# Three pieces' first FFN product by Strassen's seven block products, later maxima through DRAM, outputs waiting in the raw weights' buffer

## The chip, the cores and the metric

The kernel runs on one core of a Trainium2 chip. The metric is the time of one execution on the device, in microseconds; the median of three runs is 985.28 us (984.22 to 986.99). The profile is of one execution that took 982.83 us, of which 981.0 us are the span from its first to its last profiled instruction.

## The reference

Block-causal attention over 8 batches, 8 heads, 576 positions and head size 64, followed by a feed-forward network (FFN) on all 4608 tokens of width 512 with 2048 hidden columns:

```python
scores = scale * np.matmul(q, k.transpose(0, 1, 3, 2))
scores = np.where(block_i >= block_j, scores, -1000000000.0)
...
attn = attn / (np.sum(attn, axis=-1, keepdims=True) + 1e-09)
x = np.matmul(attn, v)
...
h = x @ w_in
g = h * np.clip(h + 3.0, 0.0, 6.0) / 6.0
return (g @ w_out).astype(np.float32)
```

## The kernel before

All of it is float32 in and out. To use TensorE's float16 rate, each operand is scaled by a power of two and split into a high and a low float16 half; a product is then three float16 products, high by high, high by low and low by high. A tensor's scale comes from its largest absolute value (`pow2_scale`, line 561). Where the maximum has to be taken over all 128 partitions (`exact`), TensorE turns the column of 128 maxima into a row (tile `mt`), VectorE (DVE) reduces it, and a second small matmul (tile `mb`) spreads the result again. This is done for each of 8 weight chunks (`w_max`, line 678) and for v of each of the 8 batches (`v_max`, line 747).

The tokens are cut into 13 pieces (line 1141), numbered 0 to 12, and a piece from 4 on has 384 tokens. Piece 0 is computed in float32. For every piece the FFN runs over 16 groups f of 128 hidden columns:

- `ffn1_` (line 1246) makes h of one f in a PSUM tile `h`: 4 depths by 3 products, each as a pair of matmuls of 64 weight columns that run side by side, so 24 matmuls of 384 columns. ScalarE (ACT) then writes `r` (a Relu), DVE multiplies, ACT writes the high half of `g` and DVE its low half.
- `ffn2_` (line 1302) adds g of one f to three PSUM accumulators `o`, 18 matmuls of 512 columns. After f = 15, the sums are scaled into tiles `osb` and stored.

Attention works on 32 pairs of heads (n). A pair is loaded, scaled and split, transposed by a DMA (`qkT`), and goes through scores (`s`), softmax on DVE and ACT (`st`, `p`, `ph`, `phl`), DMA transposes of the probabilities (`pT`), and `pv` (`pv_group`, line 1157), whose result is split into the `x` of a piece. All 4 pairs of a batch feed the pieces of that batch, so pieces 10 to 12 take batches 6 and 7.

The order of the work comes from a planner. The kernel's calls don't issue instructions; a `Recorder` (line 85) collects operations with their dependences, and each operation has a key, the time at which it is due. The keys come from tables at the top of the file: `AT` gives the due time of each attention pair, `FT` that of each FFN piece. `schedule` (line 289) then lists the operations for each engine, the smallest key first among those that could run, and chooses ACT or DVE where either can do a step (`scaled` with "AV"). The engines run these fixed lists in order. A tile whose tag has `bufs` buffers waits until an earlier tile of the tag has had its last reader.

Names that the steps below use: `raw` is the one buffer (tag `raw`, 4 KB in each partition) into which weights are loaded; `stage` has 4 buffers for short-lived tiles; `g` has 4 buffers (`NGB`); `win` holds the split weights of the first product. All operations are recorded by helpers, so that the profile gives line L491 for nearly all of them, and tiles tell them apart.

Of the kernel before, what the change touches and what calls it, by code (L numbers as in the profile page):

```python
# [8 lines left out]
F16 = mybir.dt.float16  # L9
BF16 = mybir.dt.bfloat16  # L10
# [39 lines left out]
RS, RL, VL1 = 2.209, 24.843, 24.11  # L50
VM0, VMX = 49.529, 0.186
AT = ((4, 86.25), (6, 123.23), (8, 163.76), (9, 178.32), (10, 200.46), (12, 251.25), (14, 297.48), (15, 319.97), (16, 344.82), (24, 581.69), (32, 825.86))
FT = ((0, 34), (1, 120), (2, 165.28), (3, 233.86), (4, 274.28), (5, 355.06), (7, 504.5), (10, 755.22), (13, 989.58))
UNI = False
QP = 0.558
VP = 0.387
BLK = 64
# [23 lines left out]

ADV = {("tensor", "a"): 99.24}


class Recorder:
# [11 lines left out]
    LOADS = 95.0  # L97
    BIAS = {"vector": 250.0, "gpsimd": 500.0}
    EDGE = 0.0
    BURST, PATIENCE = 3, 4000.0  # L100

    def __init__(self, nc):
        self.nc = nc
        self.ops = []
        self.key = 0.0
        self.cls = ""
        self.joint = None
        self.adv = ADV
        for n in self.NAMES:
# [6 lines left out]
    def box(a):  # L116
        sz = mybir.dt.size(a.dtype)
# [58 lines left out]
    def add(self, ways):  # L176
# [20 lines left out]
        for i, (a, w) in enumerate([(a, False) for a in ins] + [(a, True) for a in outs]):  # L197
            if self.on_chip(a):
                self.touch(op, a, w, self.LOAD[mybir.dt.size(a.dtype)] if eng == "tensor" and not i else 1.0)
# [295 lines left out]
def kernel(  # L495
# [39 lines left out]
    E_X = 2.0 ** -14  # L535
    E_G = 2.0 ** -27
    C_EXP = (D ** -0.5) * 2.0 ** -28
    C_H = 2.0 ** -28
    C_O = 2.0 ** -15 / 6.0
    TINY = 1e-18  # L540
# [5 lines left out]
    attp = ctx.enter_context(tc.tile_pool(name="att", bufs=2))  # L546
    ffp = ctx.enter_context(tc.tile_pool(name="ff", bufs=3))
    ps_s = ctx.enter_context(tc.tile_pool(name="ps_s", bufs=3, space=bass.MemoryType.PSUM))
    ps_h = ctx.enter_context(tc.tile_pool(name="ps_h", bufs=2, space=bass.MemoryType.PSUM))
# [10 lines left out]

    def pow2_scale(mx, n, nm, to=None, exact=False):
# [8 lines left out]
        if exact:  # L570
            pt_ = ps_s.tile([P, 512], F32, tag="s", name=f"mt_{nm}")
            nc.joint = "mt", nm
            for h in range(2):
                wide = mx[:, h % n:h % n + 1].to_broadcast([P, BLK])
                nc.tensor.matmul(pt_[h * BLK:(h + 1) * BLK, :P], wide, ident, start=True, stop=True)
            nc.joint = None
            dg = sm.tile([P, n + 1], F32, tag=f"dg{n}", name=f"dg_{nm}")
            nc.vector.tensor_reduce(dg[:, n:], pt_[:, :P], axis=AX.X, op=ALU.max)
            nc.vector.tensor_scalar_mul(dg[:, :n], ident[:, :(n - 1) * BLK + 1:BLK], dg[:, n:])
            mx = dg[:, :n]  # L580
        ps = ps_s.tile([P, 512], F32, tag="s", name=f"mb_{nm}")
        nc.joint = "mb", nm
        for h in range(2):
            nc.tensor.matmul(ps[h * BLK:(h + 1) * BLK, :n], ones[:, :BLK], mx, start=True, stop=True)
        nc.joint = None
        nc.vector.tensor_scalar_max(am, ps[:, :n], TINY)
# [52 lines left out]
    def w_load(w, c, half):  # L639
# [36 lines left out]
        )  # L676

    def w_max(c):

        acc = sm.tile([P, 2, 2], F32, tag="wacc", bufs=2, name=f"wacc{c}")  # L680
        for wi, w in enumerate("io"):
            for half in range(2):
                c32 = w_f32(w, c, half)
                ab = ffp.tile([P, WC], F32, tag="stage", bufs=NST_B, name=f"ab{w}{c}_{half}")
                ab = ab.rearrange("p (r l n) -> p r l n", r=c32.shape[1], l=2)
                nc.scalar.activation(ab, c32, AF.Abs, accum_out=acc[:, wi, half:half + 1])
        m = sm.tile([P, 2], F32, tag="wm", name=f"wm{c}")
        nc.vector.tensor_reduce(m, acc, axis=AX.X, op=ALU.max)
        pow2_scale(m, 2, f"w{c}", (pwio[:, c], rsio[:, c]), exact=True)

    def w_split(c):

        rs = rsio[:, c]
        for wi, w in enumerate("io"):
            for half in range(2):
                c32 = w_f32(w, c, half)
                part = w_part(w, c, half)
                hi, lo = (part[:, :, i].rearrange("p r (l n) -> p r l n", l=2) for i in range(2))
                nc.scaled(hi, c32, rs[:, wi:wi + 1], "AVP")
                nc.vector.scalar_tensor_tensor(  # L700
                    lo, c32, rs[:, wi:wi + 1], hi, op0=ALU.mult, op1=ALU.subtract
                )

# [43 lines left out]
    def v_max(n):  # L747
# [8 lines left out]
        if hp == NPAIR - 1:  # L756
            m1 = sm.tile([P, 1], F32, tag="vm1", name=f"vm1_{b}")
            nc.vector.tensor_reduce(m1, vmax[b], axis=AX.X, op=ALU.max)
            vscale[b] = pow2_scale(m1, 1, f"v{b}", exact=True)

# [11 lines left out]

    def h_scale(b):

        if b not in hs:
            t = sm.tile([P, NCH], F32, tag="sh", bufs=3, name=f"sh{b}")
# [3 lines left out]
            nc.vector.tensor_scalar_mul(t, t, C_H)  # L780
            hs[b] = t
        return hs[b]

# [373 lines left out]
    def pv_group(n, g):  # L1157
# [88 lines left out]
    def ffn1_(pc, f):  # L1246
        if pc == 0:
            return ffn1_f32(f)
        x, w, fc = xb[pc % 4], width(pc), f * P % NH
        ps = ps_h.tile([P, TP], F32, tag="h", name=f"h{pc}_{f}")  # L1250
# [51 lines left out]
    def ffn2_(pc, f):  # L1302
# [34 lines left out]
        for t, a in enumerate(acc.pop(pc)):  # L1337
            n, half = min(w - t * P, P), w - t * P < P
            o = ffp.tile([P, DM], F32, tag="stage", bufs=NST_B, name=f"osb{pc}_{t}")
            oc = o[:, :DM // 2] if half else o  # L1340
            ac = a[:, :DM // 2] if half else a
            nc.scaled(oc, ac, so[:, t:t + 1] if pc else 1.0 / 6.0, "AV")
            rows = out[row + t * P:row + t * P + n]
            if half:
# [16 lines left out]
    def ffn_step(lim):  # L1361

        nonlocal done1, done2
        if done1 < lim:
            if done1 >= NFT:
                need(done1 % NFT // 2)
            while len(n_raw) < min(4 * (done1 // 2 + 1), 4 * NCH):
                w_ops.pop(0)()
            ffn1(*divmod(done1, NFT))
            done1 += 1  # L1370
# [59 lines left out]
    for n in range(NPAIR):  # L1430
        t = RT[n]
        at(t - QR, qk_load32_rest, n, lead=RL - QR)
        at(t - QR, qk_prep32, n, 1)
        at(AS[3] + 0.1 + 0.1 * n, v_max, n)
# [93 lines left out]
```

## Time and profile before

| | before |
|---|---|
| median of 3 runs | 985.28 us (984.22 to 986.99) |
| the profiled execution | 982.83 us |
| its span | 981.0 us |
| TensorE (PE) busy | 964.2 us, 98% |
| DVE busy | 756.4 us, 77% |
| ACT busy | 696.5 us, 71% |
| granted TensorE clock, mean | 0.999 |

PE is TensorE's matmuls, PEld its weight loads, SP the engine that issues DMAs, POOL GpSimd. A group's row gives its count, its busy time, the mean duration of one in ns, and behind the second bar the idle time of its engine just before it, with what ended that. The views by windows give each engine's busy time in a stretch; the timeline and the chain give the start, the length and the count of merged instructions. Durations of back-to-back instructions overlap a little, so a count times a duration can be longer than the busy time.

### The profile page before, as it was taken

How to read it: one execution, taken by the hardware profiler on the slowest of the kernel's cores; microseconds unless marked ns; L12 is line 12 of the kernel's file. 1: busy time of each engine (PE TensorE's matmuls, PEld its weight loads, DVE VectorE, ACT ScalarE, POOL GpSimd, SP SyncE). 2: the span in 40 equal slices, each digit the busy share in tenths (PEclk: the TensorE clock that was granted, in tenths of full speed). 3: DMA queues.
4: the chain of work that ended last, by engine and by line, in shares of the span. 5: the costliest groups of instructions: out<-in, count | busy, mean ns of one | idle time of the engine just before them, and what ended most of it. 6: DMA issues, size and time to landing. Idle time of an engine off the chain costs nothing.

```text
span 981.0 us, 29087 instructions
## 1 busy us (share of the span) xinstructions
PE 964.2 (98%) x11754; PEld 722.9 (74%) x11754; DVE 756.4 (77%) x2081; ACT 696.5 (71%) x1840; POOL 28.3 (3%) x109
## 2 busy tenths in 40 slices
PE   8999999999999999999999999999999999999998
PEld 6655447877778867777777677777777777777776
DVE  6889998999989999999999898899886432332331
ACT  6899789778778888888878788787775433333332
POOL 3012000000000000000000000000000000000000
PEclk9999999999999999999999999999999999999999
DMA  6966689899898899898899898786664200000000
GB/s 141 277 204 223 159 154 178 169 183 189 155 173 148 149 175 157 170 162 148 161 186 177 151 188 156 132 164 131 108 133 77 36 34 1 1 33 1 34 2 33
DMA packets 414199, 128.91 MB, mean 131 GB/s; under 512 B 403184, under 2 KB 403440, under 8 KB 414064
## 3 DMA queue, kind: packets, MB, share of 16 engines
q1 hardware_dynamic: 414064, 127.05, 66.5%
q8 instruction: 92, 1.51, 0.6%
q14 instruction: 43, 0.35, 0.1%
HBM read 45.09 MB, written 9.44 MB: 56 GB/s over the span
## 4 chain that ended last, share of the span: by engine, by line
PE 58%; DVE 6%; DMA 2%; ACT 1%; issue 1%; DVEq 0%; ACTq 0%
PE o L491 25%; PE h L491 25%; PE s L491 4%; PE pv L491 4%; DMA pT<-ph 2%; DVE st L491 1%; DVE phl L491 1%; DVE ph L491 1%; DVE r L491 1%; DVE g L491 1%; DVE qks L491 1%; DVE vhl L491 0%; ACT p L491 0%; DVE x L491 0%; ACT r L491 0%
## 5 line engine op out<-in xcount | busy, mean ns | idle before, releaser
L491 PE MATMUL h<-x,win 128*64 128x384 f16 (+3 forms) x4790 | 440.7, 319 | 4.4 <-DVE r L491 4.4
L491 PE MATMUL o<-wout,g 128*64 128x512 f16 (+2 forms) x3424 | 432.3, 383 | 0.0
L491 PEld LDWEIGHTS <-win 128*64 128x64 f16 x4608 | 296.1, 110 | 62.5 <-issue 6.5
L491 PEld LDWEIGHTS <-g 128*64 128x64 f16 x3264 | 219.2, 110 | 91.6
L491 ACT ACTIVATE r<-h,eg,sh 128x192 f32<-128x192 f32 (+1 forms) x240 | 134.1, 580 | 115.2 <-PE h L491 110.8
L491 DVE SCALAR_TENSOR_TENSOR r<-r,eg,h 128x384 f32<-128x384 f32 (+1 forms) x192 | 110.3, 575 | 132.0 <-ACT r L491 131.3
L491 ACT ACTIVATE p<-s,st,esc 128x64 f32<-128x64 f32 (+1 forms) x280 | 163.1, 586 | 13.6 <-DVE ph L491 7.3
L491 DVE SCALAR_TENSOR_TENSOR g<-r,g 128x384 f16<-128x384 f32 (+1 forms) x192 | 99.5, 519 | 34.1 <-ACT g L491 33.3
L491 DVE TENSOR_REDUCE st<-s 128x1 f32<-128x64 f32 (+1 forms) x280 | 119.2, 446 | 6.9 <-PE s L491 6.1
L491 ACT ACTIVATE g<-r 128x384 f16<-128x384 f32 (+1 forms) x157 | 77.4, 494 | 59.2 <-DVE r L491 58.7
L491 PE MATMUL s<-qkT 128*64 128x64 f16 (+7 forms) x1120 | 101.8, 287 | 1.9 <-ACT p L491 1.3
L491 PEld LDWEIGHTS <-vhl 128*64 128x64 f16 x1680 | 74.0, 110 | 13.5 <-issue 4.1
L491 PEld LDWEIGHTS <-qkT 128*64 128x64 f16 x1120 | 62.0, 110 | 23.5 <-issue 7.6
L491 PE MATMUL pv<-pT,vhl 128*64 128x192 f16 (+2 forms) x1680 | 74.4, 233 | 1.9 <-DMA pT<-ph 0.9
L491 DVE SCALAR_TENSOR_TENSOR ph<-p,st,ph 128x256 f16<-128x256 f32 (+2 forms) x168 | 66.5, 444 | 0.1
L491 DVE SCALAR_TENSOR_TENSOR phl<-p,st,phl 128x512 f16<-128x512 f32 (+1 forms) x84 | 62.8, 789 | 0.3 <-ACT phl L491 0.3
L491 ACT ACTIVATE st<-st,esc 128x1 f32<-128x1 f32 (+2 forms) x127 | 36.8, 291 | 34.3 <-DVE st L491 32.9
L491 ACT ACTIVATION_READ_ACCUMULATOR p<-s,st,esc 128x1 f32 x280 | 55.0, 196 | 0.0
L491 ACT ACTIVATE ph<-p,st 128x64 f16<-128x64 f32 (+5 forms) x106 | 43.2, 450 | 15.8 <-DVE st L491 14.2
L491 DVE SCALAR_TENSOR_TENSOR qks<-qk,rs_q,qks 128x576 f16<-128x576 f32 x56 | 44.5, 807 | 0.1
L491 ACT ACTIVATE qks<-qk 128x576 bf16<-128x576 f32 x56 | 37.8, 677 | 0.3 <-DMA qkT<-qks 0.3
L491 ACT ACTIVATE x<-pv 128x192 f16<-128x192 f32 (+1 forms) x56 | 20.3, 363 | 11.5 <-PE pv L491 10.0
(150 smaller groups left out, 847.0 us busy)
## 6 DMA issues: line engine op xcount, KB each, us to landing
out_dram<-osb SPq DMA_DIRECT2D x35, 256.0 KB, 2.7
vnat<-in_v_dram SPq DMA_DIRECT2D x64, 128.0 KB, 3.0
qk<-in_q_dram SPq DMA_DIRECT2D x28, 288.0 KB, 3.4
qk<-in_k_dram SPq DMA_DIRECT2D x28, 288.0 KB, 4.3
rawi<-in_moe_w_in_dram SPq DMA_DIRECT2D x8, 512.0 KB, 4.5
rawo<-in_moe_w_out_dram SPq DMA_DIRECT2D x8, 512.0 KB, 4.7
ph<-in_moe_w_in_dram SPq DMA_DIRECT2D x6, 512.0 KB, 4.8
ph<-in_moe_w_out_dram SPq DMA_DIRECT2D x6, 512.0 KB, 4.0
```

Of the source, the lines that this page charges most:

```text
L491: getattr(eng, method)(*args, **kw)
```

## The change

1. **Seven products for pieces 10, 11 and 12** (`SW = 10`). For each of the 8 chunks c of 256 hidden columns (two f), the 256 x 512 weights and the 512 x 384 tokens are seen as 2 x 2 blocks, and the eight block products become seven, of sums and differences of blocks (`ffn1_seven`). Each product is 6 pairs of matmuls of 192 columns. The sums are prepared by `w_forms` (once for each chunk) and `x_forms` (once for each piece), and split into float16 halves again. The products are added up on DVE into `hh`, for which the buffers of `x1` and `ph1` serve in turn. The weights' forms `wf` live in buffers of attention (`qkT`, `pT2`, `p`), and the float32 weights `w32`, from which they are made, in the one buffer `raw`. For these pieces `pv_group` keeps x whole in float32.
2. **Outputs** `osb` of the first two of a piece's three tiles share the buffer `raw`. The very last tile is written in two halves, issued by SP and by ACT.
3. **Maxima through DRAM** (`far`) for weight chunks 3 to 7 and v of batches 1 to 7: a DMA writes the 128 maxima to DRAM, a second reads them back to every partition (`al`), and DVE reduces; the two small products `mt` and `mb` are gone there.
4. `w_max` and `w_split` take a whole half chunk (1024 elements) at a time, not 512, and no longer use GpSimd.
5. The first pair's loads of k are issued by ACT.
6. The tables of due times are new (a few lines of them below), and the calls for pieces 10 to 12 are recorded after all of attention.

```diff
-AT = ((4, 86.25), ... (24, 581.69), (32, 825.86))
-FT = ((0, 34), ... (10, 755.22), (13, 989.58))
+AT = ((4, 86.25), ... (24, 560), (32, 785))
+FT = ((0, 34), ... (10, 765), (13, 965.63))
+WFAR, VFAR = 3, 1
+SW = 10
...
     def pow2_scale(...)
+        if exact and far:
+            row = drp.tile([n, P], F32, tag=f"row{n}", name=f"dr_row_{nm}")
+            nc.sync.dma_start(row.rearrange("n p -> p n"), mx)
+            al = sm.tile([P, n, P], F32, tag="al", bufs=1, name=f"al_{nm}")
+            nc.sync.dma_start(
+                al.rearrange("p n x -> p (n x)"),
+                row.rearrange("n p -> (n p)").rearrange("(o x) -> o x", o=1).to_broadcast([P, n * P]),
+            )
+            nc.vector.tensor_reduce(am, al, axis=AX.X, op=ALU.max)
...
-                nc.sync.dma_start(
+                (nc.sync if n or not s else nc.scalar).dma_start(
                     t[:, s, :, h], src[0, 2 * n + h, :T0].rearrange("(t p) d -> p t d", p=P)
...
     def pv_group(n, g):
+            if pc >= SW:
+                nc.scaled(x_whole(pc)[:, hp, xs], ps[:, t0:t1], E_X / 4, "AV")
+                continue
...
+    def w_forms(c):
+        was, nc.key, nc.cls = (nc.key, nc.cls), WF0 + c * WFD, "w"
+        w32 = ffp.tile([P, NDT, NH], F32, tag="raw", bufs=1, name=f"w32_{c}")
+        nc.vector.tensor_add(w32, win[:, c, :, 0], win[:, c, :, 1])
...
+        for i in range(2):
...
+            s = ffp.tile([P, 2, 2, P], F32, tag="stage", bufs=NST_B, name=f"ws{c}_{i}")
+            if not i:
+                nc.vector.tensor_add(s[:, 0], a21, a22)
+                nc.vector.tensor_sub(s[:, 1], s[:, 0], a11)
+            else:
+                nc.vector.tensor_sub(s[:, 0], a11, a21)
+                nc.vector.tensor_sub(s[:, 1], a12, last[:, 1])
+            nc.scaled(o[:, :, 0], s2, 1.0, "AV")
+            nc.vector.tensor_sub(o[:, :, 1], s2, o[:, :, 0])
...
+    def x_forms(pc):
+        for r, b in ((r0, b11), (r1, x[:, 2:])):
+            nc.scaled(r[:, 0], b, 1.0, "AV")
+            nc.vector.tensor_sub(r[:, 1], b, r[:, 0])
+        for k in range(4):
+            nc.vector.tensor_sub(t, a, b)
+            nc.scaled(tt[:, k, 0], t, 1.0, "AV")
+            nc.vector.tensor_sub(tt[:, k, 1], t, tt[:, k, 0])
...
+    def ffn1_seven(pc, c):
+        def mul(o, w, x, nm):
+            for d in range(2):
+                for i, (wl, xl) in enumerate(((0, 0), (0, 1), (1, 0))):
+                    for h in range(2):
+                        nc.tensor.matmul(o[r], w[d][wl][:, r], x[d][xl], ...)
+        one_ = ps_h.tile([P, HP], F32, tag="h", name=f"u{pc}_{c}")
+        mul(one_, w11, x11, 1)
+        nc.scaled(hh[:, 5], one_, 1.0, "AV")
+        for k, runs in enumerate((
+            ((w12, x21, 2), (s2, t2, 6)), ((s1, t1, 5), (s3, t3, 7)), ((s4, x22, 3), (w22, t4, 4)),
+        )):
+            ps = ps_s.tile([P, 2, HP], F32, tag="s", name=f"u{pc}_{c}_{k}")
+            for j, run in enumerate(runs):
+                mul(ps[:, j], *run)
+            if k < 2:
+                nc.vector.tensor_add((hh[:, 0:5:4], hh[:, 1:3])[k], ps, with_)
+                if k:
+                    nc.vector.tensor_add(hh[:, 3], ps[:, 0], hh[:, 2])
+            else:
+                nc.vector.tensor_add(hh[:, 1:3], ps, hh[:, 1:3])
...
     def ffn2_(pc, f):
-            o = ffp.tile([P, DM], F32, tag="stage", bufs=NST_B, name=f"osb{pc}_{t}")
+            if t == 0:
+                pair = ffp.tile([P, 2, DM], F32, tag="raw", bufs=1, name=f"osb{pc}")
+            o = pair[:, t] if t < 2 else ffp.tile([P, DM], F32, tag="stage", bufs=NST_B, name=f"osb{pc}_{t}")
...
     def step():
-        while owed and done1 < TOT and not left[done1 // NFT]:
+        while owed and done1 < TOT and not left[done1 // NFT] and (done1 < SW * NFT or not sum(left)):
```

The order on DVE at the end of piece 9, before the change (r and g are the two DVE steps of one f, the first number is the piece, the second f):

```order
L491 SCALAR_TENSOR_TENSOR r9_14_2010<-r9_14_2010,eg_625,h9_14_2009 128x384
L491 SCALAR_TENSOR_TENSOR g9_14_2011<-r9_14_2010,g9_14_2011 128x384
L491 SCALAR_TENSOR_TENSOR r9_15_2020<-r9_15_2020,eg_625,h9_15_2019 128x384
L491 SCALAR_TENSOR_TENSOR g9_15_2021<-r9_15_2020,g9_15_2021 128x384
L491 SCALAR_TENSOR_TENSOR r10_0_2023<-r10_0_2023,eg_625,h10_0_2022 128x384
```

The same place after it (w32, ws and wf are the weights' forms of a chunk, xs, xt and xr the tokens' forms of a piece, x1<-u10 the first sum of products):

```order
L498 TENSOR_TENSOR w32_5_2112<-win_87 128x1024
L498 SCALAR_TENSOR_TENSOR r9_15_2041<-r9_15_2041,eg_598,h9_15_2040 128x384
L498 TENSOR_TENSOR xt11_2201<-xs11_2_2204,xt11_2201 128x384
L498 TENSOR_TENSOR ws5_0_2114<-w32_5_2112 128x256
L498 SCALAR_TENSOR_TENSOR g9_15_2042<-r9_15_2041,g9_15_2042 128x384
L498 TENSOR_TENSOR ws5_0_2114<-ws5_0_2114,w32_5_2112 128x256
L498 TENSOR_TENSOR ws5_1_2115<-w32_5_2112 128x256
L498 TENSOR_TENSOR ws5_1_2115<-w32_5_2112,ws5_0_2114 128x256
L498 TENSOR_TENSOR xs12_0_2279<-x0_83 128x384
L498 TENSOR_TENSOR wf5_0_2113<-ws5_0_2114,wf5_0_2113 128x2x256
L498 TENSOR_TENSOR x1_84<-u10_0_0_2130,x1_84 128x2x192
```

Between the steps of piece 9 stand forms of five and a half chunks and of pieces 10 to 12. The forms of chunks 6 and 7 follow behind the first products of piece 10.

The DMA queue at the maximum of v of batch 3, before the change:

```order
L491 DMA_TRANSPOSE pT9_1_903<-phl9_8_913 128x10x128
L491 DMA_TRANSPOSE pT10_0_922<-ph0_87 128x8x128
L491 DMA qk13_1065<-in_q_dram 128x9x64
L491 DMA_TRANSPOSE qkT11_940<-qks11_934 128x27x128
L491 DMA qk13_1065<-in_k_dram 128x9x64
L491 DMA_TRANSPOSE pT10_0_922<-ph1_88 128x18x128
```

And after it (dr_row is the row of maxima in DRAM, al its copy in every partition):

```order
L498 DMA_TRANSPOSE pT9_1_866<-phl9_8_876 128x10x128
L498 DMA dr_row_v3_1019<-vm1_3_1015 128x1
L498 DMA_TRANSPOSE pT10_0_884<-ph0_89 128x8x128
L498 DMA al_v3_1020<-dr_row_v3_1019 128x128
L498 DMA qk13_1025<-in_q_dram 128x9x64
L498 DMA_TRANSPOSE qkT11_901<-qks11_895 128x27x128
L498 DMA_TRANSPOSE pT10_0_884<-ph1_90 128x18x128
```

SP can issue al only when the row has landed; the loads and the transposes of q, k and the probabilities of pairs 10 to 13 stand behind it.

More of the change, by code (lines that the diff above doesn't have):

```diff
@@ L580, in pow2_scale @@
[L580 to L586, printed above, removed]
+            nc.vector.tensor_scalar_max(am, ps[:, :n], TINY)
         nc.vector.tensor_scalar(
@@ L676, in w_load, with w_whole @@
         )
+    def w_whole(w, c):
+        if w == "i":
+            part = win[:, c]
+            c32 = win[:, c + 1].bitcast(F32) if c + 1 < NCH else None
+        else:
+            part = wout[:, 2 * c:2 * c + 2]
+            c32 = wout[:, 2 * c + 2:2 * c + 4].bitcast(F32) if c + 1 < NCH else None
+        if c32 is None:
+            t = flat(xb[2 if w == "i" else 3], F32)[:, :2 * WC]
+            c32 = t.rearrange("p (r l n) -> p r l n", r=part.shape[1], l=2)
+        return c32, part
     def w_max(c):
-        acc = sm.tile([P, 2, 2], F32, tag="wacc", bufs=2, name=f"wacc{c}")
+        acc = sm.tile([P, 2], F32, tag="wm", name=f"wm{c}")
         for wi, w in enumerate("io"):
[L682 to L689, printed above, removed]
+            c32, _ = w_whole(w, c)
+            ab = ffp.tile([P, WC], F32, tag="stage", bufs=NST_B, name=f"ab{w}{c}")
+            ab = ab.bitcast(BF16).rearrange("p (r l n) -> p r l n", r=c32.shape[1], l=2)
+            nc.scalar.activation(ab, c32, AF.Abs, accum_out=acc[:, wi:wi + 1])
+        pow2_scale(acc, 2, f"w{c}", (pwio[:, c], rsio[:, c]), exact=True, far=c >= WFAR)
     def w_split(c):
@@ L694, in w_split @@
         for wi, w in enumerate("io"):
[L695 to L702, printed above, removed]
+            c32, part = w_whole(w, c)
+            hi, lo = (part[:, :, i].rearrange("p r (l n) -> p r l n", l=2) for i in range(2))
+            nc.scaled(hi, c32, rs[:, wi:wi + 1], "AV")
+            nc.vector.scalar_tensor_tensor(
+                lo, c32, rs[:, wi:wi + 1], hi, op0=ALU.mult, op1=ALU.subtract
+            )
     gs = []
@@ new lines, in ffn1_seven @@
+    def ffn1_seven(pc, c):
+        if not wf:
+            for k in range(NCH):
+                w_forms(k)
+        if pc not in xform:
+            x_forms(pc)
+        x11, x21, x22, t1, t2, t3, t4 = xform[pc]
+        s1, s2, s3, s4 = wf[c]
+        w11, w12, w22 = (
+            [[win[:, c, 2 * h + d, l, f * P:(f + 1) * P] for l in range(2)] for d in range(2)]
+            for f, h in ((0, 0), (0, 1), (1, 1))
+        )
+        hh = (flat(xb[1], F32)[:, :6 * HP], ph01[1].rearrange("p l u x -> p (l u x)").bitcast(F32))[c % 2]
+        hh = hh.rearrange("p (k n) -> p k n", k=6)
+        def mul(o, w, x, nm):
+            for d in range(2):
+                nc.joint = "u", pc, c, nm, d
+                for i, (wl, xl) in enumerate(((0, 0), (0, 1), (1, 0))):
+                    for h in range(2):
+                        r = slice(h * BLK, (h + 1) * BLK)
+                        nc.tensor.matmul(
+                            o[r], w[d][wl][:, r], x[d][xl],
+                            start=d == 0 and i == 0, stop=d == 1 and i == 2,
+                        )
+            nc.joint = None
+        one_ = ps_h.tile([P, HP], F32, tag="h", name=f"u{pc}_{c}")
[8 more added lines that the diff above has]
+            if k < 2:
+                with_ = hh[:, 5 - k].rearrange("p (o n) -> p o n", o=1).to_broadcast([P, 2, HP])
+                nc.vector.tensor_add((hh[:, 0:5:4], hh[:, 1:3])[k], ps, with_)
+                if k:
+                    nc.vector.tensor_add(hh[:, 3], ps[:, 0], hh[:, 2])
+            else:
+                nc.vector.tensor_add(hh[:, 1:3], ps, hh[:, 1:3])
+        eg = g_scales()[0]
+        for l in range(2):
+            r = ffp.tile([P, TP], F32, tag="stage", bufs=NST_B, name=f"r{pc}_{2 * c + l}")
+            h = hh[:, 2 * l:2 * l + 2].rearrange("p k n -> p (k n)")
+            for b, c0, c1 in spans(pc):
+                nc.scalar.activation(
+                    r[:, c0:c1], h[:, c0:c1], AF.Relu,
+                    bias=eg[:, 1, c:c + 1], scale=h_scale(b, 4.0)[:, c:c + 1],
+                )
+            nc.vector.scalar_tensor_tensor(r, r, eg[:, 2, c:c + 1], h, op0=ALU.min, op1=ALU.mult)
+            g = ffp.tile([P, 2, TP], F16, tag="g", bufs=NGB, name=f"g{pc}_{2 * c + l}")
+            nc.scaled(g[:, 0], r, 4 * E_G, "AV")
+            nc.vector.scalar_tensor_tensor(
+                g[:, 1], r, 4 * E_G, g[:, 0], op0=ALU.mult, op1=ALU.subtract
+            )
+            gt[pc, 2 * c + l] = g
@@ L1368, in ffn_step @@
                 w_ops.pop(0)()
+            while done1 >= SW * NFT and not done1 % 2 and done2 < done1 + 2 - NGB:
+                ffn2(*divmod(done2, NFT))
+                done2 += 1
             ffn1(*divmod(done1, NFT))
```

148 lines of the change are left out of this document (104 added, 44 removed).

## The prediction

> **What bounds the kernel now.** I read the page first: which engine is busy, and where.
>
> ```profile
> span 981.0 us, 29087 instructions
> PE 964.2 (98%) x11754; PEld 722.9 (74%) x11754; DVE 756.4 (77%) x2081; ACT 696.5 (71%) x1840; POOL 28.3 (3%) x109
> PE   8999999999999999999999999999999999999998
> DVE  6889998999989999999999898899886432332331
> PE 58%; DVE 6%; DMA 2%; ACT 1%; issue 1%; DVEq 0%; ACTq 0%
> ```
>
> PE is busy in every slice, and the chain that ends last runs mostly on it. DVE is nearly as full until slice 30 and idles afterwards. Busy matmuls need not stream at full rate, so I went on to the windows (busy us of each engine, the count in brackets) and to the chain in order of time.
>
> ```profile
> 100.00:200.00 100.00, 98.20 (x1229) 63.13 (x1227) 95.67 (x292) 84.22 (x226) 2.94 (x12) 1.00 0.87 163
> 290.00:300.00 10.00, 6.88 (x136) 5.91 (x132) 6.32 (x29) 6.90 (x21) 0.00 (x0) 1.00 0.80 174
> 300.00:400.00 100.00, 99.95 (x1453) 78.29 (x1451) 92.42 (x263) 85.02 (x233) 1.21 (x8) 1.00 0.92 155
> 716.00:786.00 70.00, 69.58 (x868) 54.38 (x866) 45.83 (x117) 39.85 (x101) 0.30 (x2) 1.00 0.47 84
> 786.00:848.00 62.00, 62.00 (x673) 47.02 (x669) 19.40 (x36) 20.46 (x34) 0.00 (x0) 1.00 0.04 14
> 848.00:910.00 62.00, 62.00 (x673) 47.12 (x670) 19.11 (x33) 24.18 (x50) 0.00 (x0) 1.00 0.04 14
> 910.00:972.00 62.00, 62.00 (x670) 46.98 (x668) 19.05 (x33) 20.49 (x34) 0.00 (x0) 1.00 0.04 14
> ```
>
> ```profile
> 784.58 1.95 PE h L491 x24
> 788.48 1.95 PE h L491 x24
> 969.48 6.49 PE o L491 x60
> ```
>
> A window's row has its length, PE, PEld, DVE, ACT and POOL with their counts, the granted clock (1.00 throughout), and DMA's share and rate. Piece 9 takes about 716 to 786, and pieces 10, 11 and 12 take 62 us each. There PE is busy without a gap, with 3.90 us from one f to the next, half of it h and half o, and DVE uses 19 of 62 us. So PE's column count sets the time of the last 190 us: what is taken from h there comes off the end, if its inputs are ready. In piece 9, attention still shares DVE.
>
> **The seven products.** Per chunk, before: 2 f of 24 matmuls, 2 x 1.95 = 3.90 us. After: 7 products of 6 pairs of 192 columns. Pieces 1 and 3 already run this shape, shown here ahead of a 384-column row of the same timeline:
>
> ```profile
> 282.04 1.18 PE L491 MATMUL h<-x,win 128*64 128x192 f16 x24
> 784.39 2.14 PE L491 MATMUL h<-x,win 128*64 128x384 f16 x24
> L491 PEld LDWEIGHTS <-win 128*64 128x64 f16 x4608 | 296.1, 110 | 62.5 <-issue 6.5
> ```
>
> The timeline's 2.14 us are 0.19 longer than the chain's 1.95, which is the last matmul running out. So 12 pairs of 192 take 1.18 - 0.19 = 0.99 us, 82 ns a pair; 42 pairs take 3.47 us. That saves 0.43 us a chunk, 10.4 us over 24 chunks. By columns alone an eighth of 3.90, 11.7 us, is the other bound. I take 10.4.
>
> **The maxima.** Each costs PE the stream time of mt and mb, from a start to the next instruction's start:
>
> ```profile
> 108.15 0.40 PE L491 MATMUL mt_w<-ident,wm 128*64 128x128 f32 x4
> 108.37 2.77 PE L491 MATMUL h<-x,win 128*64 128x384 f32 x16
> 110.95 0.25 PE L491 MATMUL mb_w<-dg_w,one 128*64 128x2 f32 x4
> 111.03 2.79 PE L491 MATMUL o<-wout,g 128*64 128x512 f32 x12
> ```
>
> 0.22 + 0.08 = 0.30 us, twelve times: 3.6 us saved, or nothing if PE waits there for DVE anyway.
>
> **Head and tail.**
>
> ```profile
> 0.73 0.99 SPq L491 DMA_DIRECT2D qf<-in_q_dram  x2
> 1.76 1.02 SPq L491 DMA_DIRECT2D qf<-in_k_dram  x2
> 3.94 1.83 PE L491 MATMUL qt<-ident,qf 128*128 128x128 f32 x6 [3.94 <-DMA qf<-in_q_dram]
> 976.05 1.98 ACT L491 ACTIVATE osb<-o,so 128x512 f32<-128x512 f32 x3 [4.60 <-PE o L491]
> 976.76 1.63 SPq L491 DMA_DIRECT2D out_dram<-osb  x3
> ```
>
> PE first waits 3.94 us for q and k. With k issued by ACT at the same time as q, it is issued 1.03 us earlier, so I take 1.0 us (0 to 1.0, if v or the next pair becomes the late one). The last of three osb takes 1.98 / 3 = 0.66 us; in two halves on two engines it takes about 0.2 less, and the store behind it carries half the bytes: 0.2 us (0 to 0.5).
>
> **What DVE gets, and whether PE waits for it.** The prices, from same-sized DVE rows (two forms of g give 1.07 ns per element), and a group that shows how neighbours overlap:
>
> ```profile
> L491 DVE SCALAR_TENSOR_TENSOR g<-r,g 128x384 f16<-128x384 f32 x160 | 88.5, 553 | 33.6 <-ACT g L491 32.8
> L491 DVE SCALAR_TENSOR_TENSOR g<-r,g 128x192 f16<-128x192 f32 x32 | 11.0, 348 | 0.6 <-ACT g L491 0.4
> L491 DVE TENSOR_TENSOR rd<-ident,sums 128x192 f32<-128x192 f32 x12 | 4.3, 356 | 0.1
> L491 DVE SCALAR_TENSOR_TENSOR r<-r,eg,h 128x384 f32<-128x384 f32 x160 | 97.5, 609 | 127.2 <-ACT r L491 126.7
> L491 DVE SCALAR_TENSOR_TENSOR x<-pv,x 128x192 f16<-128x192 f32 x52 | 18.1, 350 | 1.2 <-PE pv L491 0.9
> L491 DVE SCALAR_TENSOR_TENSOR ph<-p,st,ph 128x256 f16<-128x256 f32 (+2 forms) x168 | 66.5, 444 | 0.1
> ```
>
> By that slope 256 elements cost 0.42 us, 512 cost 0.69, 768 cost 0.96 and 1024 cost 1.24. The 168 ph steps sum to 74.6 us and keep DVE busy for 66.5, so neighbours overlap by 0.05 us each.
>
> In pieces 11 and 12, a chunk adds four sums (0.55 + 0.55 + 0.35 + 0.55 = 2.0 us) to 2 x (0.61 + 0.55) = 2.3. That is 4.3 us of DVE in 3.47 + 3.90 = 7.37 us of PE, and the g of a chunk are used only after the next chunk's products, so these stay hidden. Without that distance, each chunk would show its chain of about 3 us.
>
> Piece 9 is different. In the new order DVE has there, between r of f = 0 and the first sum of piece 10, 6 w32 (7.4 us), 24 ws (10.1), 11 wf lows (7.6), 7 xs and 8 xt lows (8.3) and 5 or 6 smaller ones (3.0), 36 us in all; of piece 9's stretch, 7 low halves of x are gone (7 x 0.35 = 2.5). With the 45.8 us of before this makes 79 us. PE has 70 us there, 3.9 more for the two o that now go ahead of piece 10, and 1.5 for its first products: 75 us. Taking off 0.05 us for each of some 170 instructions leaves DVE 71 us, so it is full and PE waits somewhat. From below this is 0. From above, DVE at its best share of a window, 95.67%, needs 79 / 0.957 = 83, that is 8 us of waiting. I take 3. Behind it, o0 and o1 of piece 10 need the sums of piece 9 moved into osb, which wait for `raw` until w32 of chunk 7 has been read. The order puts the products of four chunks (13.9 us), the last o of piece 9 (3.9) and four early o2 (2.6) ahead of them, 20 us of cover for some 25 us of DVE steps of which the first few are done earlier; this is inside the 3 us.
>
> Early on, nine of the sixteen high halves of the weights go to DVE, as whole 1024s. DVE was busy 95.67% there. I take 1 us, between 0 and 3. POOL loses eight instructions, and nobody waits for it.
>
> The new due times change who waits where. PE loses 3.1 us at 290 to 300, and such a gap may close or open. I take 0, between -4.7 and +4.7.
>
> **The sum**, against the profiled 982.83 us: -10.4 - 3.6 - 1.0 - 0.2 + 3 + 1 = -11.2, which gives 971.6. The median of the runs lies 2.45 us above the profiled one, so 974.1.
>
> **The rivals.**
>
> *Nearly no change.* DVE works at its usual share, 92.42%, in piece 9: 79 / 0.924 = 85.5, 10.5 us late, and 3 early. For it speaks that dependences leave even the fullest windows some idle time; against it, that DVE idles for 24 of 70 us there now, and that its forms wait for nothing but weights. 982.83 - 15.2 + 13.5 + 2.45 = 983.6, within 0.3% (3 us, about what a measurement of this kernel can tell from no change).
>
> *More than I forecast.* The columns give 11.7, nothing waits for DVE, and the gap at 290 closes with some of its like (4.7): 982.83 - 11.7 - 3.6 - 1.5 - 4.7 + 2.45 = 963.8. For it: PE's idle gaps before 300 hang on order alone.
>
> *Slower by the round trip through DRAM.* DVE and SP stop in order: DVE at the reduction of al, SP at al's issue, with transposes behind it.
>
> ```profile
> out_dram<-osb SPq DMA_DIRECT2D x35, 256.0 KB, 2.7
> qkT<-qks SPq DMA_TRANSPOSE x28, 7.6
> ```
>
> Between v's maximum and that reduction stand 30 DVE instructions for batch 3, some 12 us at the 0.4 of the ph row. Two transfers at the output's 2.7 us are 5.4 and hidden. If both take the longest of the page's medians, 7.6, they need 15.2, and each maximum stops DVE for 3.2. DVE stops from 6 us a transfer on; at 7 us the seven maxima of v cost 7 x 2 = 14 us, which turns the sign. At 7.6 us they cost 22.4: 974.1 + 22.4 = 996.5. Against it: the new rows of 128 numbers are far smaller than that transpose. By the Trainium skill (DMA: Bandwidth & Descriptors, Anatomy of one DMA) a DMA has a fixed cost of about 2.0 us; told for the GpSimd path; two would be an estimated 4, hidden too. No run here shows such a small one yet.
>
> *Slower because weight loads bind.* A load's row has 110 ns. If a pair of 192 took that long, 42 pairs would be 4.62 us against 3.90, 24 x 0.72 = 17.3 us lost in place of 10.4 gained: 974.1 + 27.7 = 1001.8. It is excluded as far as the 192-column row above holds for this stream, too. By the Trainium skill (TensorE: Matmul & The Clock Gate, LDWEIGHTS) a load takes its columns divided by 1.2 in ns, 53 for 64 columns. Two in a row would be an estimated 107 ns a pair and the sum 14 us worse than before; the trace, with 82 ns a pair, says that the two overlap, and the measurement decides. That the seven products hold more work than seven eighths is no rival: 42 pairs of 192 are 8064 columns, against 24 of 384, 9216.
>
> **How the numbers follow.** The forecast 0.67; more than that 0.14; nearly no change 0.12 (0.02 of it over the line to slower); the round trip 0.05; weight loads 0.02. The range takes the forecast with its bounds and the first two rivals, 963.8 to 983.6. Faster is 0.67 + 0.14 = 0.81, same 0.10, slower 0.02 + 0.05 + 0.02 = 0.09.
>
> **What would show it.** Right: chunks of pieces 11 and 12 follow each other every 7.37 us (7.80 before); u tiles show 82 ns a pair; no mt or mb after the third chunk and the first batch; PE starts near 2.9 us; PE's idle time around the start of piece 10 is 3 us, ended by DVE tiles ws, wf, xt or by osb. Wrong: a chunk takes 7.8 us or more, am_v is ended by a DMA for microseconds, or PE idles over 8 us between 716 and 830.

## The result, and the profile after

The change made the kernel slower: 1027.64 us (median of 4 runs, 1021.16 to 1032.00) against 985.58, a ratio of 1.042 (95% interval 1.036 to 1.048). The forecast was 974.1 us, with 963.8 to 983.6 as its range. The profiled execution took 1025.14 us, its span 1023.3, the mean granted clock was 0.981.

The page of the kernel after: the engines, PE's 40 slices and its granted clock in tenths.

```profile
span 1023.3 us, 30730 instructions
PE 966.3 (94%) x12490; PEld 698.6 (68%) x12490; DVE 842.2 (82%) x2238; ACT 706.6 (69%) x1828; POOL 18.6 (2%) x101
PE   7996979988999998999899999979999999999998
PEclk9998989999999998999999999989999999999999
```

PE has holes in the first 28 slices, where it had hardly any before, and the clock dips with some of them; the last 12 slices are full. So the end, with its seven products, is not where the time went. The pace there is what the forecast said it would be, 8 x 7.37 = 59.0 us a piece; these are the two stretches of 59 us that hold pieces 11 and 12, of 960 matmuls each (62 us each before):

```profile
897.00:956.00 59.00, 59.00 (x964) 48.02 (x962) 37.46 (x74) 31.05 (x62) 0.00 (x0) 1.00 0.04 15
956.00:1015.00 59.00, 59.00 (x964) 48.02 (x962) 35.13 (x66) 22.83 (x42) 0.00 (x0) 1.00 0.05 16
```

The holes come where a maximum goes through DRAM: of the eleven that are longer than 1.5 us, ten begin 9 to 18 us after SP has issued a row. One of them, on SP's timeline of the kernel after (start, length, operation):

```profile
383.22 0.54 SPq L498 DMA_DIRECT2D dr_row_v<-vm  x1
383.81 0.42 SPq L498 DMA_DIRECT2D qk<-in_q_dram  x1
384.28 0.69 SPq L498 DMA_DIRECT2D qk<-in_k_dram  x1
386.14 10.43 SPq L498 DMA_TRANSPOSE pT<-ph  x1
396.67 0.53 SPq L498 DMA_DIRECT2D al_v<-dr_row_v  x1
```

And the same place on PE's timeline:

```profile
389.68 1.63 PE L498 MATMUL h<-x,win 128*64 128x384 f16 x18
392.93 0.82 PE L498 MATMUL o<-wout,g 128*64 128x512 f16 x6
398.30 1.49 PE L498 MATMUL pv<-pT,vhl 128*64 128x192 f16 x18 [4.55 <-DMA pT<-ph]
400.81 3.14 PE L498 MATMUL h<-x,win 128*64 128x384 f16 x18
```

The row goes out at 383.22. The transpose behind it occupies SP for 10.43 us, and PE runs dry for 4.55 us until that transpose has landed. Then PE runs slower for a while: 18 matmuls of h take 3.14 us against 1.63 ahead of the hole. The windows of that stretch show the granted clock (the number behind POOL's bracket):

```profile
386.00:396.00 10.00, 7.75 (x106) 5.23 (x103) 9.18 (x26) 6.78 (x19) 0.00 (x0) 1.00 0.79 63
396.00:406.00 10.00, 7.70 (x66) 5.72 (x67) 3.10 (x13) 4.01 (x13) 0.00 (x0) 0.66 1.01 160
406.00:416.00 10.00, 10.00 (x141) 7.65 (x139) 10.00 (x25) 6.41 (x19) 0.30 (x2) 1.00 1.02 184
```

So this hole costs twice: as idle time, then at a clock of 0.66 on average. The holes of 2.43 and 3.40 us in the same run, before 299 and 590 us, were followed by a clock of 1.00. The list of DMA issues (count, KB each, median us from issue to landing) has what is new:

```profile
al_w<-dr_row_w SPq DMA_DIRECT2D x5, 128.0 KB, 5.5
al_v<-dr_row_v SPq DMA_DIRECT2D x7, 64.0 KB, 3.6
dr_row_v<-vm SPq DMA_DIRECT2D x7, 0.5 KB, 9.5
dr_row_w<-wm SPq DMA_DIRECT2D x5, 1.0 KB, 10.6
```

The smallest transfers, of half a kilobyte and one, take the longest. (These medians stand on few rows: the profile knows the landing of two of the seven of v, 8.3 and 10.7 us, and of one of the five of the weights.) And pT, the transposes of ph, before and after (ns: shortest, median, longest):

```profile
L491 SPq DMA_TRANSPOSE pT<-ph x56: 1232/2612/4059, 121.2 to 755.0; - x56
```

```profile
L498 SPq DMA_TRANSPOSE pT<-ph x56: 1231/2413/10427, 139.6 to 809.6; - x56
```

The median is as it was; the longest has grown from 4.06 to 10.43 us.

### The profile page after: what moved, and what is told of

Same layout as the page of the kernel before. It is cut to its first block, busy times and chain, and to the rows that moved or that the text cites. A ratio compares the mean times of both kernels' runs of the same rounds, so it can differ in the third digit from the quotient of the medians.

```text
span 1023.3 us, 30730 instructions
## 1 busy us (share of the span) xinstructions
PE 966.3 (94%) x12490; PEld 698.6 (68%) x12490; DVE 842.2 (82%) x2238; ACT 706.6 (69%) x1828; POOL 18.6 (2%) x101
## 5 line engine op out<-in xcount | busy, mean ns | idle before, releaser
L498 PE MATMUL o<-wout,g 128*64 128x512 f16 (+3 forms) x3410 | 423.9, 383 | 0.3 <-ACT osb L498 0.3
L498 PE MATMUL h<-x,win 128*64 128x384 f16 (+3 forms) x3648 | 338.6, 322 | 5.8 <-DVE r L498 3.6
L498 PEld LDWEIGHTS <-win 128*64 128x64 f16 x4320 | 242.2, 111 | 65.3 <-issue 8.8
L498 PEld LDWEIGHTS <-g 128*64 128x64 f16 x3264 | 207.4, 110 | 108.3 <-DVE g L498 0.9
L498 ACT ACTIVATE p<-s,st,esc 128x64 f32<-128x64 f32 (+1 forms) x280 | 162.8, 586 | 10.7 <-DVE ph L498 4.8
L498 ACT ACTIVATE r<-h,eg,sh 128x192 f32<-128x192 f32 (+1 forms) x176 | 98.3, 579 | 29.4 <-PE h L498 26.8
L498 ACT ACTIVATE g<-r 128x384 f16<-128x384 f32 (+1 forms) x145 | 71.7, 495 | 46.6 <-DVE r L498 42.7
L498 DVE SCALAR_TENSOR_TENSOR r<-r,eg,h 128x384 f32<-128x384 f32 (+1 forms) x144 | 80.8, 561 | 16.4 <-ACT r L498 16.2
L498 PEld LDWEIGHTS <-qkT 128*64 128x64 f16 x1120 | 57.7, 113 | 45.5 <-issue 18.0
L498 ACT ACTIVATE ph<-p,st 128x256 f16<-128x256 f32 (+5 forms) x112 | 45.6, 454 | 8.1 <-DVE st L498 5.1
L498 PEld LDWEIGHTS <-wf 128*64 128x64 f16 x1152 | 49.0, 110 | 0.3
```

The costliest lines, as they stand in the source:

```text
L498: getattr(eng, method)(*args, **kw)
```

## The experiments

**First question: which part of the change.** Theory A was the trip of the maxima through DRAM; theory B the new due times, or a VectorE overfull with the forms. All maxima back on the chip:

```
-WFAR, VFAR = 3, 1
+WFAR, VFAR = 8, 8
```

> All maxima are found on the chip, as before the change (no row in DRAM); the seven products, the new due times and the whole-tile weight preparation stay. Theory A (the trip of the maxima through DRAM holds SyncE, what is queued behind comes late and TensorE idles and then runs at a lower clock): 975 to 980 us, with a granted clock back at 0.99 to 1.00 and no idle stretch of TensorE near 390, 480 and 580 us. Theory B (the new due times or a VectorE that is overfull): it stays above 1010 us and the idle stretches stay.

Measured: 972.5 us (971.9 to 973.33), 0.987 of before (0.985 to 0.988). No seven products, maxima through DRAM:

```
-SW = 10
+SW = 13
```

> The first product of the last three pieces is made of the eight plain block products as before; the maxima still go through DRAM. Theory A: the tail gives back what it gained, 4.0 us a piece for three pieces, so 1027.6 + 12 = about 1039 us. Theory B (the forms of the seven products overload VectorE): near 985 us.

Measured: 1052.81 us, 1.067 (1.064 to 1.071), 14 us more than theory A expected. Both edits together:

> Neither the seven products nor the trip through DRAM: what is left of the change is the new due times, the weight preparation over whole tiles, the k loads on ScalarE's queue at the head and the output that waits in the raw weights' buffer. Theory A: 983 to 991 us, the time before within 0.6%, and 10 to 13 us above the kernel with the maxima on the chip and the seven products. Theory B: above 1000 us.

Measured: 981.67 us, 0.996 (0.994 to 0.997). Theory B falls: with the maxima on the chip again the rest of the change gains 13 us. 9.2 of these are the seven products (981.67 to 972.5), 4.0 the rest (985.66 to 981.67). The trips cost 1027.6 - 972.5 = 55 us. Between the two profiled spans lie 1023.3 - 970.3 = 53.0 us: PE idles 41.8 us longer, and it is busy 11.2 us longer, with fewer matmuls. Without the seven products the trips cost 71, so their price hangs on what stands beside them.

**Which trips.**

```
-WFAR, VFAR = 3, 1
+WFAR, VFAR = 8, 1
```

> The whole change, but only the seven maxima of v go through DRAM; those of the weights are found on the chip. If each trip costs alike (about 55 us above the kernel without trips, in twelve), seven cost 32 us: about 1005 us. If the early ones, while the weights are prepared, cost nothing, about 1027 us; if only they cost, about 973 us.

Measured: 1027.94 us (1025.66 to 1029.89). The other way round, `WFAR, VFAR = 3, 8`:

> The whole change, but only the five late maxima of the weights go through DRAM; those of v are found on the chip. If each trip costs alike, five cost 23 us: about 995 us. With the run that has only the seven of v, the two losses should add up to about 55 us if the trips are independent.

Measured: 1000.57 us (998.74 to 1002.74). The seven of v alone cost 55 us, the five of the weights alone 28, and both together not 83 but 55. The trips are not independent: the first of v and the last of the weights fall into the same 50 us, and the planner lays out another order each time. What a single one costs is not settled by these two.

**Second question: is it the waiting?** I first took it to be that: SP or DVE stands at the trip, and what is queued behind comes late. The waits are there: in the kernel after, SP stands 32.5 us in all for rows and 5.0 for a broadcast. The planner counts a store's landing as lasting 4137 - 1860 = 2277 ns, plus its bytes by a rate, and the rows took 9.5 us and more. Two kernels went at the waiting. One moves both DMAs to GpSimd's queue:

```
-            nc.sync.dma_start(row.rearrange("n p -> p n"), mx)
+            nc.gpsimd.dma_start(row.rearrange("n p -> p n"), mx)
...
-            nc.sync.dma_start(
+            nc.gpsimd.dma_start(
                 al.rearrange("p n x -> p (n x)"),
```

> The whole change, but the row and its broadcast are issued by GpSimd's queue instead of SyncE's. Theory A, first form (SyncE stands still at the broadcast until the row has landed, and transposes and loads queue behind it): most of the loss is gone, 975 to 990 us, and the transposes pT and qkT are issued on time. Second form (the 4-byte pieces of the row slow the DMA engines for every transfer): the time stays above 1010 us and the transposes near the rows still take 6 us and more.

Measured: 1049.53 us, 1.064 (1.058 to 1.071). Its rows of v land after 11.2 us (the median of the two known) and its transposes of phl, now nowhere behind a row on their queue, still have one that takes 10.7:

```profile
dr_row_v<-vm POOLq DMA_DIRECT2D x7, 0.5 KB, 11.2
dr_row_w<-wm POOLq DMA_DIRECT2D x5, 1.0 KB, 10.3
```

```profile
L498 SPq DMA_TRANSPOSE pT<-phl x84: 1232/1332/10668, 173.5 to 850.9; - x84
```

The other tells the planner of a later landing, so that the steps that wait stand further down in the order:

```
-                o.end = dma + tail
+                o.end = dma + tail + (LAND if any(x.startswith("dr_") for x in o.tiles) else 0.0)
```

with `LAND = 8000.0` (ns).

> The whole change with its trips through DRAM, but the planner counts 8 us more until such a row or its broadcast has landed, so that SyncE's broadcast and VectorE's maximum stand later in the order, behind other work. Form one of theory A (the planner counts about 2.3 us for a landing that takes 7 to 12, so engines stand at the wait in the middle of other work): 973 to 985 us, with no wait over 3 us for a row or a broadcast. Form two (small pieces slow the DMA engines): it stays above 1010 us.

Measured: 1033.11 us, 1.048 (1.044 to 1.052), no better than the change, although SP now waits 0.9 us in all for rows and broadcasts and DVE not at all. Then the decisive one, with the maxima found on the chip and the rows written all the same, for nobody:

```
             nc.sync.dma_start(row.rearrange("n p -> p n"), mx)
+        if False:
             al = sm.tile([P, n, P], F32, tag="al", bufs=1, name=f"al_{nm}")
...
         else:
             if exact:
```

> The maxima are found on the chip (972.5 us without more), and each row of 4-byte pieces is still written to DRAM by SyncE, twelve times, but nothing reads it and nothing waits for it. Form one of theory A (the loss is the waiting: whichever engine stands at the row or at its broadcast holds what is queued behind it): 972 to 977 us, and the rows may well take 7 to 12 us to land. Form two (the small pieces slow the DMA engines for the transposes beside them): over 990 us, with transposes of 6 us and more beside each row.

Measured: 1041.11 us (1038.86 to 1042.79), 1.057 (1.053 to 1.060): the whole loss and more, 68.6 us above the 972.5 without rows, and nothing reads a row. (Why it is 13 us slower than the change itself I did not take apart; mt and mb, 3.6 us by the forecast, are a part of it.) My theory of the waiting falls. SP's and then PE's timeline of this kernel show how it comes about:

```profile
400.18 0.54 SPq L498 DMA_DIRECT2D dr_row_v<-vm  x1
400.77 0.44 SPq L498 DMA_DIRECT2D qk<-in_q_dram  x1
401.26 0.59 SPq L498 DMA_DIRECT2D qk<-in_k_dram  x1
401.96 14.06 SPq L498 DMA_TRANSPOSE pT<-ph  x1
```

```profile
408.75 0.82 PE L498 MATMUL o<-wout,g 128*64 128x512 f16 x6
418.02 1.49 PE L498 MATMUL pv<-pT,vhl 128*64 128x192 f16 x18 [8.45 <-DMA pT<-ph]
```

SP passes the row in 0.54 us and issues two loads at once; it stands for 14.06 us in the next transpose, and PE loses 8.45 us for lack of it. The row does not hold its reader but the transfers beside it. By the packet records of the trace the row's pieces all start between 401.26 and 401.54 us, about a microsecond behind the issue; it is 256-byte packets of the others, begun after them, that take up to 6.3 us each, where the median of all is 0.02 and the longest in the kernel without rows 2.2.

**Third question: what about the row does it.** All of these write rows for nobody, as the last kernel. In the traces of all but the one with wide pieces, SP, ACT, DVE and GpSimd run the same operations in the same order as there, so that these kernels differ in the rows' pieces alone. Each 4-byte piece on its own 512 bytes:

```
-            row = drp.tile([n, P], F32, tag=f"row{n}", name=f"dr_row_{nm}")
-            nc.sync.dma_start(row.rearrange("n p -> p n"), mx)
+            row = drp.tile([n, P, P], F32, tag=f"row{n}", name=f"dr_row_{nm}")
+            nc.sync.dma_start(row[:, :, 0].rearrange("n p -> p n"), mx)
```

> As the run with the rows that nobody reads (twelve rows written aside, 1041.1 us against 972.5 without them), but each 4-byte piece goes to its own 512 bytes in DRAM instead of 128 pieces side by side in 512 bytes. If the loss comes from pieces of different DMA engines that meet in the same few lines of DRAM: 973 to 985 us. If any 4-byte piece that is written to DRAM costs it: 1025 to 1050 us.

Measured: 970.86 us (970.19 to 971.59), 0.986 (0.984 to 0.987): no cost at all. The rows land in a quarter of the time, and no transpose of ph takes over 4.7 us:

```profile
dr_row_v<-vm SPq DMA_DIRECT2D x7, 0.5 KB, 2.3
dr_row_w<-wm SPq DMA_DIRECT2D x5, 1.0 KB, 2.6
```

```profile
L498 SPq DMA_TRANSPOSE pT<-ph x56: 1231/2210/4674, 121.8 to 754.7; - x56
```

Against the rows side by side, where the landing of one row of v and of one of the weights is known:

```profile
dr_row_v<-vm SPq DMA_DIRECT2D x7, 0.5 KB, 10.4
dr_row_w<-wm SPq DMA_DIRECT2D x5, 1.0 KB, 10.9
```

Wide pieces, 512 bytes each, side by side:

```
+            wide = sm.tile([P, P], F32, tag="wide", bufs=1, name=f"wide_{nm}")
+            nc.vector.tensor_scalar_mul(wide, ident, mx[:, :1])
+            nc.sync.dma_start(row, wide)
```

with `row` of 128 by 128 numbers, 64 KB.

> As the run with the rows that nobody reads, but each of the 128 partitions writes 512 bytes side by side (64 KB in all, the same number of pieces; VectorE spreads the maximum over them first, about 0.2 us each of twelve). If it is the small size of a piece that costs: 973 to 980 us. If it is any write to DRAM between the transposes (the order of a write and a transpose on the queue): 1025 to 1050 us.

Measured: 986.53 us (985.36 to 989.48), between the two expectations. The rows land after 3.0 (v) and 2.1 us. The last g of piece 9 stands at 784.41 us against 783.75 without rows: up to there twelve writes cost 0.7 us. The other 14 us or so are lost where piece 10 begins, with one wait of PE (total, times, longest):

```profile
PE o L498 <- ACT g L498: 11.3, 1, 11.3
```

No row is written there, so this belongs to the order that the planner made, not to the rows; why this order waits there I did not try. Only 16 of the 128 pieces:

```
-            nc.sync.dma_start(row.rearrange("n p -> p n"), mx)
+            nc.sync.dma_start(row[:, :16].rearrange("n p -> p n"), mx[:16])
```

> As the run with the rows that nobody reads, but of each row only the pieces of the first 16 partitions are written (an eighth of the 4-byte pieces). If the cost goes by the number of pieces: 68.6 us / 8 = 9 us above the kernel without rows, about 981 us. If one such write costs by itself, however few its pieces: 1025 to 1050 us.

Measured: 972.17 us (971.19 to 974.11): nothing. Then the distance and the number. 64 bytes apart, `row` as `[n, P, 16]`:

> Rows that nobody reads, with the maxima on the chip, the 4-byte pieces 64 bytes apart instead of side by side (1041.1 us) or 512 bytes apart (970.9 us). If the clash is within 64 bytes: 969 to 975 us. If it is within 512 bytes: 1000 us and more.

Measured: 971.56 us (970.38 to 972.83). 16 bytes apart, `[n, P, 4]`:

> The same, 16 bytes apart, so that four pieces share 64 bytes and 32 share 512. If pieces that share 64 bytes clash: between 975 and 1041 us, by their number per 64 bytes (a quarter of the extra cost would be 990 us). If not: 969 to 975 us.

Measured: 971.19 us (970.2 to 973.99). Side by side, the first 64 partitions:

> The same with the pieces side by side, but only those of the first 64 partitions, so four lines of 64 bytes instead of eight. By the number of pieces: 1007 us. If it sets in with a number above 64, as it did not with 16: 970 to 975 us. If it sets in between 16 and 64 and then stays: 1030 us and more.

Measured: 1002.94 us (1001.95 to 1008.12). In one view each, the weights' rows (two at a time) of the last two kernels; the second is the median of two known landings:

```profile
dr_row_w<-wm SPq DMA_DIRECT2D x5, 1.0 KB, 3.9
```

```profile
dr_row_w<-wm SPq DMA_DIRECT2D x5, 0.5 KB, 7.2
```

So neither the size of a piece nor their number does it alone: 128 pieces of 4 bytes cost nothing at 16 bytes' distance, and 16 cost nothing side by side. 64 side by side cost (1002.9 - 972.5) / 12 = 2.5 us a write, and 128 cost 5.7 (a write of the weights holds two rows). It could be that many small pieces next to each other in DRAM are written one behind the other, but the landings give no fixed time for each: one write of 128 pieces took 10.4 us, one of 2 x 128 took 10.9, and 16 side by side landed after 2.0, no later than 128 apart. Pieces that start 16 bytes from each other did not hold each other up, neither those of 4 bytes here nor those of 16 further down, and pieces that start 4 bytes from each other did; where between them the border lies the runs do not show. By the Trainium skill (DMA: Bandwidth & Descriptors, Specifications) the DMA does a read-modify-write for transfers below 512 bytes; as far as that goes, all 4-byte pieces should pay alike, and the measurement says that they do not. Why others wait for them, the same page (Queues, rings and completion order) offers a reason: a DMA's count on its semaphore lands only after all earlier writes of that DMA engine, whatever queue they came from. That GpSimd's queue did not help agrees with it, but a late count does not explain packets that themselves take up to 6.3 us; no run here looks at a single DMA engine, and how the pieces slow the others stays open.

**Last question: did the waiting cost anything?** The forecast had hidden it. The whole change, with pieces 512 bytes apart (`rows_` holds a space for each of the twelve, which GpSimd's queue clears at the start):

```
-            row = drp.tile([n, P], F32, tag=f"row{n}", name=f"dr_row_{nm}")
-            nc.sync.dma_start(row.rearrange("n p -> p n"), mx)
+            row = rows_[nm]
+            nc.sync.dma_start(row[:, :, 0].rearrange("n p -> p n"), mx)
...
-                row.rearrange("n p -> (n p)").rearrange("(o x) -> o x", o=1).to_broadcast([P, n * P]),
+                row.rearrange("n p x -> (n p x)")[:n * P].rearrange("(o x) -> o x", o=1).to_broadcast([P, n * P]),
```

> The whole change with its trips and its waits, but each 4-byte piece of a row goes to its own 512 bytes; the broadcast then reads as many bytes as in the change from the start of that space, so only one or two partitions' maxima are in it and the scales are not those of the whole tensor (cleared to zero at the start by GpSimd's queue). If the waiting is hidden, as the prediction had it: 972.5 less up to 12 x 0.30 us for the maxima that leave TensorE, 967 to 973 us. If standing at the trip costs by itself, some of it in each of twelve places: 980 us and more.

Measured: 980.89 us (979.75 to 981.98). From 20 us on its windows are nearly full, but PE's first products of the scores (`sf`) start late:

```profile
16.24 0.70 PE L498 MATMUL mt_v<-ident,vm 128*64 128x128 f32 x4 [7.99 <-DVE vm L498]
17.14 1.70 PE L498 MATMUL sf<-qkf 128*128 128x128 f32 x6
```

In the kernel without trips they start at 7.43. The reason stands in GpSimd's timeline of the same run, the clearing of the rows ahead of a tile of q and k:

```profile
2.73 2.52 POOL L498 DMA_DIRECT2D dr_row_w<-zeros  x5
5.25 3.34 POOL L498 DMA_DIRECT2D dr_row_v<-zeros  x7
8.62 0.57 POOL L498 MEMSET qkf<- 64x576 f32 x1
```

So the loss there was of my own making. The same with the clearing issued by SP and due at 30 us:

```
-        nc.gpsimd.dma_start(
+        nc.sync.dma_start(
```

> As the run with the whole trip and pieces 512 bytes apart (980.9 us), but the rows are cleared by SyncE's queue during the first 70 us instead of GpSimd's at the start; the scales again see only one or two partitions. If the late start was the whole loss there: 980.9 - 9.7 = about 971 us. If waiting for the trip costs: still 978 us and more.

Measured: 969.06 us (968.7 to 970.73), 0.985 (0.982 to 0.987). The twelve trips cost nothing that can be seen when their rows land quickly: SP's waits for them come to 0.2 us in all. Without these mt and mb the kernel is even 3.4 us faster than the one with the maxima on the chip, or 2.2 when each is taken against the kernel before as measured beside it (984.44 and 985.66 us). Its order is one of its own, so not all of this need be mt and mb. A complete version for v, with the weights on the chip, writes each maximum four times:

```
+            fat = sm.tile([P, n, 4], F32, tag="fat", bufs=1, name=f"fat_{nm}")
+            nc.vector.tensor_copy(fat, mx.rearrange("p (n o) -> p n o", o=1).to_broadcast([P, n, 4]))
...
+            nc.sync.dma_start(row.rearrange("n p x -> p n x"), fat)
```

> The whole computation: the maxima of v go through DRAM as in the change, but each partition writes its maximum four times, 16 bytes, so that a row is 128 pieces of 16 bytes side by side (2 KB), and the broadcast reads all of it; the weights' maxima are found on the chip. If the clash goes by the number of pieces within a stretch of DRAM and the trip is hidden: 972.5 - 7 x 0.30 = 970.4 us. If side by side is what counts, whatever the size: 1000 us and more.

Measured: 975.99 us (974.93 to 976.63), 0.991 (0.989 to 0.993). Its rows, 128 pieces of 16 bytes side by side, land in 2.7 us, so the clash is gone there too, yet it stays 3.5 us behind the kernel with all maxima on the chip. Its last g of piece 1 is already 3.5 us later (204.8 against 201.3), an order of its own in the first 200 us; I did not take that apart. Of the complete versions that with all maxima on the chip is the fastest, 972.5 us, better than both kernels.

## Why the prediction was wrong, step by step

**Seven products: right.** Predicted 42 pairs in 3.47 us and chunks every 7.37. In the kernel with the maxima on the chip:

```profile
854.77 4.08 PE L498 MATMUL o<-wout,g 128*64 128x512 f16 x36
858.66 1.18 PE L498 MATMUL u<-xr,win 128*64 128x192 f16 x24
859.65 1.68 PE L498 MATMUL u<-xt,wf 128*64 128x192 f16 x36
861.13 0.69 PE L498 MATMUL u<-xr,wf 128*64 128x192 f16 x12
861.63 0.69 PE L498 MATMUL u<-xt,win 128*64 128x192 f16 x12
862.12 4.08 PE L498 MATMUL o<-wout,g 128*64 128x512 f16 x36
```

From 858.66 to 862.12 are 3.46 us for 84 matmuls, from one o to the next 7.35. Taking out these products alone made 9.2 us, 10.4 were forecast. The rival of the weight loads falls by this.

**DVE full in piece 9: right that it is full, wrong that PE waits.** The same kernel's window of piece 9, and that of piece 10:

```profile
716.00:786.00 70.00, 70.00 (x886) 45.53 (x884) 69.74 (x166) 52.42 (x127) 0.30 (x2) 1.00 0.50 87
786.00:848.00 62.00, 61.80 (x1022) 49.90 (x1018) 49.58 (x101) 26.00 (x49) 0.00 (x0) 1.00 0.04 15
```

DVE is busy 69.74 of 70 us, and PE loses 0.2 us in the two windows, not 3. The kernel with the wide pieces, which lost some 14 us at the same place in an order of its own, suggests that this cover is thin.

**Head: wrong.** PE was to start near 2.9 us and starts at 4.65 instead of 3.94:

```profile
4.65 1.51 PE L498 MATMUL qt<-ident,qf 128*128 128x128 f32 x6 [4.65 <-POOL qkf L498]
```

The row names GpSimd's clearing of a tile, but that ended at 4.66 us, and PE had begun to load its first weights at 4.62. In the kernel with the whole trip and the pieces 512 bytes apart, GpSimd was done with its one tile at 2.78 us, and PE starts no earlier; the row there names k:

```profile
4.72 1.52 PE L498 MATMUL qt<-ident,qf 128*128 128x128 f32 x6 [4.72 <-DMA qf<-in_k_dram]
```

So k is still the likely cause. In the kernel with the maxima on the chip its second load is issued 1.04 us earlier than before, but it lands at 4.52 us in place of 4.76, and the second of q at 4.13 in place of 3.80. Two steps failed: the row of before says that its 3.94 us were waited for q, not for q and k; and a load that was issued a microsecond earlier, beside another, did not land a microsecond earlier. It is 0.7 us lost for 1.0 forecast.

**Due times, the rest: inside its bounds.** The forecast took head, tail, early DVE and due times at -0.2 together, with 4.7 either way for the due times; without products and trips the kernel gained 4.0.

**Maxima: the saving is about right.** 3.6 forecast, 972.5 - 969.06 = 3.4 measured once the rows don't clash, 2.2 against the kernels before beside them. With pieces apart, and scales from one or two partitions, the change takes 969.1 us, inside the range but 5 us below the 974.1 forecast: the 3 us of waiting did not come, and head, tail, early DVE and due times gained 4.0 in place of 0.2. That the sum is near is in part luck.

**The round trip: the step that failed.** The rival had the sign and gave it 0.05. Two sentences of it went wrong. "Against it: the new rows of 128 numbers are far smaller than that transpose" sized a landing by its bytes; 512 bytes took 9.5 us (two landings known), longer than any median that the prediction had looked at. And its price was that of DVE stopping at the reduction, with 996.5 us at the worst. By that way of counting, a row of 9.5 us and a broadcast of 3.6 would stop DVE for 1.1 us, seven times, 8 us of the 55. But the loss came without any waiting (1041.1 us with rows that nobody reads), it stayed where the waits were gone (1033.1), and the trip with a quick row is hidden, as the forecast said (969.1). The forecast put at nothing what a row does to the transfers beside it, and there the price was paid: transposes of up to 14.06 us for which PE waits, 5.7 us a write. An operation that no row of before shows was looked at for how long it takes, not for what it does to its neighbours. By the Trainium skill (DMA: Bandwidth & Descriptors, Anatomy of one DMA) a DMA has a fixed cost of about 2.0 us, told for the GpSimd path; the rows with their pieces apart agree with 2.3, the rows side by side, with 9.5 to 10.4, do not. The signs of being wrong that were named ahead were of little use: chunks came every 7.35 us, am_v was ended by a DMA once, for 7.4 us, and PE idled not between 716 and 830 but before.

## What to carry to other kernels

A column of one number per partition written side by side into DRAM is a poor neighbour: it made the DMA transposes beside it wait 10 us and more, whoever issued it and whether or not anyone read it. Give such pieces a distance (16 bytes were enough here), widen them, or turn the column on TensorE for 0.3 us. When a change adds a kind of transfer that the kernel has not had, price what it does to the transfers around it, and test that by the transfer alone, with no reader.

## What the runs showed of the hardware

- 128 writes of 4 bytes side by side in DRAM: 10.4 us to land (one landing known in that run, two of 8.3 and 10.7 in the kernel after); 512 bytes apart 2.3 us; 64 side by side in each of two rows 7.2 (two known), 128 in each of two 10.9 (one known).
- In the two places shown, a transpose of ph issued behind such a row occupies SP for 10.4 and 14.1 us (the median in the kernel after is 2.4), while plain loads between the two are issued in 0.4 to 0.7 us each.
- A hole of PE of 4.55 us, up to 398.30 us, stands in a stretch from 396 to 406 us with a mean granted clock of 0.66, in which 18 matmuls of 384 columns took 3.14 us in place of 1.63.
